# A filler that hands over from one part to the next within one request

## The chip, the cores and the metric

The kernel runs on one core of a Trainium2 chip. The core has five engines, each with its own instruction stream, which it works through in the order in which it was written: TensorE (PE; its weight loads are listed apart, as PEld), VectorE (DVE), ScalarE (ACT), GpSimd (POOL) and SyncE (SP). The metric is the device time of one execution in microseconds (us); lower is better.

## The reference

Attention over 2 batches of 8 heads (576 positions of 64), in which only scores within `tau` of a row's largest are kept; its output `x` (1152 rows of 512) goes through a first mixture of 8 experts and then a second of 4, each expert a hidden layer of 1024 with ReLU. Every expert sees every row:

```
scores = scale * np.matmul(q, k.transpose(0, 1, 3, 2))
thresh = np.max(scores, axis=-1, keepdims=True) - tau
scores = np.where(scores >= thresh, scores, -1000000000.0)
...
P = np.exp(logits)
for _ in range(8):
    P /= P.sum(1, keepdims=True) + 1e-09
    P /= P.sum(0, keepdims=True) + 1e-09
    P *= N / E
for e in range(E):
    h = np.maximum(x @ w1[e], 0.0)
    ye = h @ w2[e]
    out += P[:, e:e + 1] * ye
```

## The kernel before, in words

Everything is in one program, which writes each engine's instructions in a fixed order by hand. Products are taken in pieces: a float is split into a high part (`xh`, `wh`, `hh`, made by a cast on ACT) and the rest (`xl`, `wl`, `hl`, made by a subtract on DVE or POOL), and three products of such parts are summed.

**Attention.** 72 units of 128 query rows go through a pipeline; `Attention.step` writes one step of it: turns (transposes, L327 and L329) of the unit two steps back, the mask of the current one (L309 on DVE), the exponentials (L305 on ACT), `fill(0, ...)`, scores of the unit two steps on (L282), in some steps the product with the values (L383, L385), `fill(1, ...)`, and `side()`, which cooks weights: a cast on ACT (L107) and a subtract on POOL (L109) per tile. Units 0 to 15 and 16 to 35 belong to batch 0, the others to batch 1 (9 steps per pair of heads). Queries for a later head are prepared on ACT and POOL too (L252 to L257).

**The fill.** Once batch 0 is finished, its rows go through experts 0 and 1 of the first mixture while attention goes on for batch 1. `expert_fill` is a generator, called a part here: it yields after every few matmuls. A part covers 256 rows ("near") or 320 rows ("far"). First come 8 blocks, one per tile `ft` of the hidden layer: 12 matmuls into a bank of PSUM (L536), then `hh` on ACT (L542) and `hl` on DVE (L545), for a far part also copies of its edge columns on POOL (L549). A block takes three requests. Then for each 128 rows a product of 24 matmuls (L564), two to a request, whose bank is copied out at its end (L568). There are two banks for this and for the values' product. `todo` holds the parts in order: expert 0 near and far, expert 1 near and far. `pull(n)` takes `n` requests from the first; `fill` gives 3 in its first half of a step and the rest of a block (or 4 in all in the later products) in its second.

**After the attention** `todo` gets the near and far part of expert 1 for the first half of batch 1's rows ("chunk 2"), and a loop runs until `todo` is empty. An iteration has one `pull(3)`, and by its number `n`: from 18 on three ticks, in which POOL and ACT prepare weights for the main stage (sums L829, splits L80 and L85); up to 7, and then each third, a step of `gate()` (the mixture's weights: a small product on PE, L908, and eight small operations on DVE, L909 to L913 and L902 to L905); in the others sums of rows on DVE (L957 to L966), and, when the gate is done, two operations of `scale()` (L933, L935), which multiply the accumulators `acc` by these weights.

**The main stage** does all the rest by products of seven units per half expert. Its first half's units are taken in the order 1, 7, 6, 4, 5, 2, 3; unit 1 takes `xh` and `xl`, units 7, 6 and 4 take `xth` and `xtl`, made on ACT and DVE (L80, L85) at its start, and all are on PE's L1132. Operations of `scale()` that the loop has not got to are done in the main stage's slots.

Of the kernel before, what the change touches and what calls it, by code (L numbers as in the profile page):

```python
# [29 lines left out]
def attention_two_moe_kernel(ctx, tc, qP, kP, qT, kT, vp, tau, wg, w1, w1s, w2, w2s, dp, m2w1s, m2w2, m2w2s, out):  # L30
# [6 lines left out]
    def pool(stack, name, bufs=1, **kw):  # L37
        return stack.enter_context(tc.tile_pool(name=name, bufs=bufs, **kw))
# [39 lines left out]
    def split(eh, el, hi, lo, src):  # L78
        if eh is A:
            A.copy(hi, src)  # L80
        elif eh is V:
            V.tensor_copy(hi, src)
        else:
            G.tensor_scalar(hi, src, 1.0, 1.0, op0=ALU.mult, op1=ALU.mult)
        el.tensor_tensor(lo, src, f(hi), op=ALU.subtract)  # L85
# [6 lines left out]
    def fetch(n):  # L92
        while len(raws) < n and tiles:
            w, e, ft = tiles.pop(0)
            raw = rp.tile([P, DM], F32, tag="raw", name="raw", bufs=3)
            nc.sync.dma_start(raw, w[e, :, ft])
            raws.append(raw)

    def cook(later=None):

        k = 1 + len(cooked) // FT % 2
        if not len(cooked) % FT and len(cooked) < 2 * FT:
            gap(wp, 192 if k == 1 else 64)
        hi = wp.tile([P, DM], F32R, tag=f"w{k}h", name="wh", bufs=FT)
        lo = wp.tile([P, DM], F32R, tag=f"w{k}l", name="wl", bufs=FT)
        raw = raws.pop(0)
        A.copy(hi, raw)  # L107
        if later is None:
            G.tensor_tensor(lo, raw, f(hi), op=ALU.subtract)  # L109
        else:  # L110
            later.append(lambda: V.tensor_tensor(lo, raw, f(hi), op=ALU.subtract))
        cooked.append((hi, lo))
# [481 lines left out]
    with ExitStack() as att:  # L594
        ap = pool(att, "attn", side="right")
        ps_s = Ring([whole_psum[:, k:k + 2] for k in (0, 2)])
        ps_t = Ring([whole_psum[:, 4].rearrange("p (a b) -> p a b", a=4)])
        ps_r = Ring([whole_psum[:, 5]])
        banks.pool = ps = Some([whole_psum[:, k] for k in (6, 7)])
        at = Attention(ap, ps_s, ps_t, ps_r, ps)  # L600
        for p in range(H // 2):
            at.add_pair(0, p, 0, 256, True, p == 0)
        nA0 = len(at.units)
        for p in range(H // 2):
            at.add_pair(0, p, 256, 320, False)
        nA1 = len(at.units)
        for p in range(H // 2):
            at.add_pair(1, p, 0, S, False)
        at.plan()
        room = [2 * FT]  # L610
        at.load()
        drop = on[:, 0:1]
        V.tensor_scalar(drop, tau_sb, 0.0, None, op0=ALU.is_ge)
        V.tensor_scalar(esc, drop, 0.125, None, op0=ALU.mult)
        V.tensor_scalar(lin[:, 0:1], drop, -0.125, None, op0=ALU.mult)
        V.tensor_scalar(drop, drop, -BIG, BIG, op0=ALU.mult, op1=ALU.add)
        V.scalar_tensor_tensor(lin[:, 1:2], tau_sb, 8.0, drop, op0=ALU.mult, op1=ALU.add)
        V.tensor_tensor(drop, tau_sb, drop, op=ALU.add)
        V.tensor_scalar(on[:, 1:2], drop, -1.0, None, op0=ALU.mult)

        def side():
            if at.t >= -1:
                fetch(2)
            if at.t >= nA0 - 3 and raws and room[0] and (at.t % 3 < 2 if at.t < nA1 else room[0] > 2 or at.t % 2):
                room[0] -= 1
                cook()
            if at.t == 20:
                nc.sync.dma_start(wg_sb, wg)
                nc.sync.dma_start(dp_sb, dp)
            if at.t == 24:  # L630
                split(V, V, wg2[:, :, :E1], wg2[:, :, E1:], wg_sb)

        def free(n):
            room[0] += n

        X0, X1 = Expert(0), Expert(1)
        near, far = ((0, 0), (1, P)), ((2, 32), (3, 32 + P))
        todo = [(nA0 + 4, expert_fill(hp, X0, 0, 256, near, acc, None, 0, at.later, keep)),
                (nA1 + 3, expert_fill(hp, X0, 256, 320, far, acc, tail0[0], 0, at.later, free)),
                (nA1 + 3, expert_fill(hp, X1, 0, 256, near, y1, None, 0, at.later, keep)),  # L640
                (nA1 + 3, expert_fill(hp, X1, 256, 320, far, y1, tail0[1], 0, at.later, keep))]

        left, spent = [0], [0]
        few = dict(zip(range(nA1 - 3, nA1 + 4), (2, 2, 2, 2, 2, 1, 1)))

        def pull(n, end=True):

            for i in range(n):
                if not todo or at.t <= todo[0][0] or (left[0] == 1 and not end):
                    return i  # L650
                left[0] = next(todo[0][1], -1)
                if left[0] < 0:
                    todo.pop(0)
                if left[0] <= 0:
                    left[0] = 0
                    return i + 1
            return n

        def fill(phase, busy):
            if phase == 0:  # L660
                if 0 <= at.t < nA0 - 3 and at.t % 2 == 0:
                    room[0] -= 1
                    cook()
                spent[0] = pull(few.get(at.t, 3))
            elif left[0] or not busy:
                pull(max(few.get(at.t, RA1 if at.t < nA1 + 3 else RA2) - spent[0], 0), True)

        while at.step(fill, side):
            pass
        at.flush()  # L670
        while left[0]:
            pull(1)
        at.flush()
        while raws:
            cook()
            fetch(2)
# [917 lines left out]
```

## Time and profile before

| what | value |
|---|---|
| median of 3 runs (lowest to highest) | 1287.18 us (1287.1 to 1287.38) |
| the profiled execution's own time | 1286.37 us |
| its span | 1284.6 us |
| PE, PEld busy | 1267.8 us (99%), 1207.6 us (94%) |
| DVE, ACT, POOL busy | 880.5 us (69%), 736.4 us (57%), 897.7 us (70%) |
| bytes read, written | 69.86 MB, 2.36 MB |

The span is what the profiler saw from the first to the last instruction; the execution's own time has 1.8 us more around it. Busy time is the union of an engine's instructions. A row of a timeline gives start, length, engine, line of the kernel and operation; instructions of one kind that follow each other stand as one row with their count, and a bracket tells how long the engine had been idle before it and on whom it waited. In stretches the granted clock is a share of full speed.

### The profile page before, as it was taken

How to read it: one execution, taken by the hardware profiler on the slowest of the kernel's cores; microseconds unless marked ns; L12 is line 12 of the kernel's file. 1: busy time of each engine (PE TensorE's matmuls, PEld its weight loads, DVE VectorE, ACT ScalarE, POOL GpSimd, SP SyncE). 2: the span in 40 equal slices, each digit the busy share in tenths (PEclk: the TensorE clock that was granted, in tenths of full speed). 3: DMA queues.
4: the chain of work that ended last, by engine and by line, in shares of the span. 5: the costliest groups of instructions: out<-in, count | busy, mean ns of one | idle time of the engine just before them, and what ended most of it. 6: DMA issues, size and time to landing. Idle time of an engine off the chain costs nothing.

```text
span 1284.6 us, 25109 instructions
## 1 busy us (share of the span) xinstructions
PE 1267.8 (99%) x9373; PEld 1207.6 (94%) x9373; DVE 880.5 (69%) x1851; ACT 736.4 (57%) x1483; POOL 897.7 (70%) x987
## 2 busy tenths in 40 slices
PE   8998999999999999999999999999999999999998
PEld 5597988888889999999999999999989999999998
DVE  6888888666637666666666666666745666666667
ACT  6887887423446555555655555566546465555553
POOL 7997987405796767867776786777668568677770
PEclk9999999999999999999999999999999999999999
DMA  5542330101221112211111221111212012111102
GB/s 171 161 125 78 97 98 17 42 1 34 79 70 51 42 42 58 58 34 51 50 42 42 58 59 34 50 51 42 58 36 61 20 51 58 35 58 50 42 18 74
DMA packets 43225, 73.84 MB, mean 57 GB/s; under 512 B 5216, under 2 KB 12512, under 8 KB 43104
## 3 DMA queue, kind: packets, MB, share of 16 engines
q1 hardware_dynamic: 42816, 71.96, 19.4%
q8 instruction: 74, 1.21, 0.4%
q14 instruction: 47, 0.39, 0.1%
q10 hardware_dynamic: 288, 0.28, 0.1%
HBM read 69.86 MB, written 2.36 MB: 56 GB/s over the span
## 4 chain that ended last, share of the span: by engine, by line
PE 87%; DVE 5%; POOL 3%; issue 2%; ACT 2%; DMA 0%; SPq 0%; DVEq 0%; POOLq 0%; ACTq 0%
PE mm L1132 34%; PE mm L1444 33%; PE mm L564 5%; PE mm L536 5%; PE mm L282 2%; PE mm L1252 2%; PE mm L327 2%; DVE ex L309 1%; PE mm L376 1%; POOL wl L85 1%; DVE st L287 1%; PE mm L385 1%; DVE etl L358 1%; PE mm L383 1%; ACT ex L305 1%
## 5 line engine op out<-in xcount | busy, mean ns | idle before, releaser
L85 POOL TENSOR_TENSOR wl<-raw,wh 128x512 fp32r<-128x512 f32 x217 | 282.9, 1310 | 179.8 <-ACT wh L80 166.6
L1232 DVE SCALAR_TENSOR_TENSOR acc<-mm,p,acc 128x256 f32<-128x256 f32 (+1 forms) x428 | 195.3, 508 | 72.2 <-PE mm L1444 59.3
L1444 PE MATMUL mm<-wh,h 128*128 128x256 f32 x960 | 173.3, 279 | 0.0
L1139 ACT COPY snap<-mm 128x576 f32<-128x576 f32 x126 | 80.9, 642 | 157.1 <-DVE mm L1293 77.9
L80 ACT CAST wh<-raw 128x512 fp32r<-128x512 f32 x217 | 133.5, 627 | 47.3 <-PE mm L1444 26.4
L1444 PEld LDWEIGHTS mm<-wh,h 128*128 128x128 f32 x960 | 146.5, 188 | 0.0
L1132 PE MATMUL mm<-xh,wl 128*128 128x288 f32 x672 | 145.7, 298 | 0.3
L1132 PE MATMUL mm<-xh,wh 128*128 128x288 f32 x672 | 143.3, 294 | 0.0
L1132 PE MATMUL mm<-xl,wh 128*128 128x288 f32 x672 | 143.0, 294 | 0.0
L1444 PE MATMUL mm<-wl,h 128*128 128x256 f32 x480 | 134.5, 280 | 0.1
L1444 PE MATMUL mm<-wh,tails 128*128 128x256 f32 x696 | 126.1, 279 | 0.0
L85 POOL TENSOR_TENSOR wl<-sum,wh 128x512 fp32r<-128x512 f32 x82 | 107.1, 1307 | 8.2 <-ACT wh L80 8.1
L1132 PEld LDWEIGHTS mm<-xh,wl 128*128 128x128 f32 x672 | 106.3, 188 | 3.1 <-DVE mm L1152 0.5
L1132 PE MATMUL mm<-xth,wl 128*128 128x288 f32 x504 | 108.1, 295 | 0.1
L1132 PE MATMUL mm<-xtl,wh 128*128 128x288 f32 x504 | 107.7, 294 | 0.0
L1132 PE MATMUL mm<-xth,wh 128*128 128x288 f32 x504 | 107.5, 294 | 0.0
L1132 PEld LDWEIGHTS mm<-xl,wh 128*128 128x128 f32 x672 | 107.5, 188 | 0.0
L1132 PEld LDWEIGHTS mm<-xh,wh 128*128 128x128 f32 x672 | 107.3, 188 | 0.0
L1444 PEld LDWEIGHTS mm<-wh,tails 128*128 128x128 f32 x696 | 106.2, 188 | 0.0
L80 ACT CAST wh<-sum 128x512 fp32r<-128x512 f32 x82 | 51.5, 628 | 85.4 <-POOL sum L829 71.9
L1444 PE MATMUL mm<-wl,tails 128*128 128x256 f32 x348 | 97.2, 279 | 0.0
L1444 PEld LDWEIGHTS mm<-wl,h 128*128 128x128 f32 x480 | 90.1, 188 | 0.5 <-issue 0.3
(242 smaller groups left out, 3487.8 us busy)
## 6 DMA issues: line engine op xcount, KB each, us to landing
raw<-in_w1s SPq DMA_DIRECT2D x56, 256.0 KB, 2.6
raw<-in_w2s SPq DMA_DIRECT2D x48, 256.0 KB, 2.6
raw<-in_w SPq DMA_DIRECT2D x40, 256.0 KB, 3.2
raw<-in_m2w1s SPq DMA_DIRECT2D x32, 256.0 KB, 2.6
raw<-in_m2w2s SPq DMA_DIRECT2D x28, 256.0 KB, 2.7
kr<-in_kT SPq DMA_DIRECT2D x22, 288.0 KB, 3.0
vr<-in_vp SPq DMA_DIRECT2D x24, 160.0 KB, 2.3
qr<-in_qT SPq DMA_DIRECT2D x8, 288.0 KB, 2.9
```

The lines of the kernel that those rows point to most:

```text
L80: A.copy(hi, src)
L85: el.tensor_tensor(lo, src, f(hi), op=ALU.subtract)
L282: T.matmul(sc[:m, hf, :HS], lhsT=q, rhs=kk[:, hf * HS:(hf + 1) * HS], start=i == 0, stop=i == len(ops) - 1)
L287: V.tensor_reduce(st[:, 0:1], u["sc"][:, :, :HS], axis=AX.XY, op=ALU.max, negate=not u["q"][0][0]["ws"])
L327: T.transpose(et[:, kt], exf[:, kt * P:(kt + 1) * P], ident)
L536: T.matmul(ph[:, :n], lhsT=a[:, kt * P:(kt + 1) * P], rhs=x[:, kt, n0:n0 + n], start=i == 0 and kt == 0, stop=i == 2 and kt == KT - 1)
L564: T.matmul(py, lhsT=x, rhs=a, start=i == 0, stop=i == 3 * FT - 1)
L1132: T.matmul(ch[b][:, g, :HS], lhsT=w[:, (2 * g + kt) * P:(2 * g + kt + 1) * P], rhs=operand(u, kt, lo), start=first and j == 0, stop=j == l ...
L1139: A.copy(v[u], m)
L1232: V.scalar_tensor_tensor(a, src, s, a, op0=ALU.mult, op1=ALU.add)
L1252: T.matmul(py, lhsT=hid[x][:, kk, o:o + P], rhs=w[y], start=n == 0, stop=n == 3 * HF - 1)
L1444: T.matmul(m, lhsT=hid(x, kt + ko), rhs=wk[y], start=first and n == 0, stop=n == 5, skip_group_check=True)
```

## The change

Only `pull` is changed. When a part is at its end, its generator gives nothing more. Before, this was found out by a request, which was thereby used up, and `pull` returned. Now `pull` takes the part off `todo` and asks the next one within the same request, if that one's time has come. (The test of `end` goes too; no caller leaves it at a value at which it matters.)

```
         def pull(n, end=True):
 
             for i in range(n):
-                if not todo or at.t <= todo[0][0] or (left[0] == 1 and not end):
-                    return i
-                left[0] = next(todo[0][1], -1)
-                if left[0] < 0:
-                    todo.pop(0)
+                left[0] = -1
+                while left[0] < 0:
+                    if not todo or at.t <= todo[0][0]:
+                        left[0] = 0
+                        return i
+                    left[0] = next(todo[0][1], -1)
+                    if left[0] < 0:
+                        todo.pop(0)
                 if left[0] <= 0:
                     left[0] = 0
                     return i + 1
             return n
```

No instruction is added or removed, but many move. Lines behind the change have numbers higher by 3 in the changed program (L568 and before keep theirs). The first move is on PE, in step 40, between the turn of one unit and the scores of another; rows with a plus are new at their place, with a minus they stood there before.

```order
 L327 MATMUL mm_95<-ident_68,ex_1591 128x128 x4
 L329 MATMUL mm_95<-ident_68,ex_1591 64x128
+L536 MATMUL mm_95<-xh_90,wl_186 128x320 x4
+L536 MATMUL mm_95<-xl_91,wh_185 128x320 x4
+L536 MATMUL mm_95<-xh_90,wh_185 128x320 x4
 L282 MATMUL mm_95<-kh_1525,qs_1565 128x288 x2
 L282 MATMUL mm_95<-kl_1526,qs_1565 128x288 x2
```

The first block of the far part of expert 0 stands one step earlier than before; steps 55 and 70 get a block in the same way. The parts that follow a step 55 are two steps earlier, those that follow a step 70 three.

In the loop after the attention, ACT's order at the far part of chunk 2. Before:

```order
L80 CAST wh_3720<-raw1_3297 128x512
L80 CAST wh_3725<-raw3_3299 128x512
L568 COPY acc5_3282<-mm_95 128x512
L80 CAST wh_3739<-sum0_3301 128x512
L542 ACTIVATE hh_3765<-mm_95 128x320
L542 ACTIVATE hh_3785<-mm_95 128x320
L542 ACTIVATE hh_3805<-mm_95 128x320
L542 ACTIVATE hh_3834<-mm_95 128x320
```

And in the changed program, the fifth to the eighth block of the same part:

```order
L542 ACTIVATE hh_3819<-mm_95 128x320
L80 CAST wh_3827<-raw1_3342 128x512
L80 CAST wh_3832<-raw3_3344 128x512
L542 ACTIVATE hh_3851<-mm_95 128x320
L80 CAST wh_3859<-sum0_3346 128x512
L542 ACTIVATE hh_3876<-mm_95 128x320
L542 ACTIVATE hh_3905<-mm_95 128x320
```

The same casts stood ahead of all eight blocks and now stand between them; the cast of `sum0` is ahead of the seventh block's `hh`.

At the seam of the loop and the main stage, DVE's order behind the last scalings. Before (`acc8` is what the loop's last product is copied to):

```order
L935 SCALAR_TENSOR_TENSOR acc3_64<-y1_101,p1_86,acc3_64 128x512
L933 TENSOR_SCALAR acc7_3284<-acc7_3284,p1_86 128x512
L568 COPY acc8_3285<-mm_95 128x512
L933 TENSOR_SCALAR acc8_3285<-acc8_3285,p1_86 128x512
L85 TENSOR_TENSOR xtl_4039<-sums_3289,xth_4038 128x288 x6
```

And in the changed program:

```order
L936 TENSOR_SCALAR acc5_3327<-acc5_3327,p1_86 128x512
L568 COPY acc8_3330<-mm_95 128x512
L936 TENSOR_SCALAR acc6_3328<-acc6_3328,p1_86 128x512
L936 TENSOR_SCALAR acc7_3329<-acc7_3329,p1_86 128x512
L936 TENSOR_SCALAR acc0_61<-acc0_61,p1_86 128x512
L938 SCALAR_TENSOR_TENSOR acc0_61<-y1_101,p1_86,acc0_61 128x512
L936 TENSOR_SCALAR acc1_62<-acc1_62,p1_86 128x512
L938 SCALAR_TENSOR_TENSOR acc1_62<-y1_101,p1_86,acc1_62 128x512
L85 TENSOR_TENSOR xtl_4034<-sums_3334,xth_4033 128x288 x6
```

Between the copy of `acc8` and the six subtracts `xtl` stood one scaling and now stand six; five more follow behind `xtl`.

## Rows read from the trace of the kernel before

**Rows 1.** The page: busy time, the chain that ended last, POOL's largest group

```profile
PE 1267.8 (99%) x9373; PEld 1207.6 (94%) x9373; DVE 880.5 (69%) x1851; ACT 736.4 (57%) x1483; POOL 897.7 (70%) x987
...
PE 87%; DVE 5%; POOL 3%; issue 2%; ACT 2%; DMA 0%; SPq 0%; DVEq 0%; POOLq 0%; ACTq 0%
...
L85 POOL TENSOR_TENSOR wl<-raw,wh 128x512 fp32r<-128x512 f32 x217 | 282.9, 1310 | 179.8 <-ACT wh L80 166.6
```

**Rows 2.** Stretches: length, busy PE, PEld, DVE, ACT, POOL, clock, DMA, GB/s

```profile
126.89:157.40 30.51, 29.63 (x218) 29.36 (x219) 27.41 (x71) 26.00 (x59) 27.80 (x53) 1.00 0.28 80
...
241.10:321.85 80.75, 80.75 (x478) 70.96 (x478) 49.68 (x140) 22.20 (x56) 27.45 (x63) 1.00 0.09 30
```

**Rows 3.** PE's waits from 120 to 242 us: total, times, longest

```profile
PE mm L282 <- DVE ex L309: 1.5, 2, 1.0
PE mm L327 <- DVE etl L358: 1.5, 3, 0.9
```

**Rows 4.** Timeline of step 40

```profile
126.69 0.57 ACT L568 COPY acc<-mm 128x512 f32<-128x512 f32 x1
...
127.77 0.53 PE L282 MATMUL mm<-kh,qs 128*128 128x288 f32 x2 [1.03 <-DVE ex L309]
```

**Rows 5.** Timeline of step 64: PE's product, the last weights' subtract

```profile
209.72 0.39 PE L564 MATMUL mm<-wh,hl 128*128 128x512 f32 x1
...
210.25 1.29 POOL L109 TENSOR_TENSOR wl<-raw,wh 128x512 fp32r<-128x512 f32 x1
```

**Rows 6.** The chain that ended last, 284 to 300 us

```profile
283.94 3.43 PE mm L564 x15
...
290.36 0.17 PE mm L908 x2
290.53 5.33 PE mm L536 x36
```

**Rows 7.** Timeline of chunk 2's far blocks

```profile
294.62 0.62 ACT L80 CAST wh<-sum 128x512 fp32r<-128x512 f32 x1 [2.77 <-POOL sum L829]
...
295.15 1.18 ACT L542 ACTIVATE hh<-mm 128x320 fp32r<-128x320 f32 x3
...
295.62 1.29 DVE L545 SCALAR_TENSOR_TENSOR hl<-mm,hh 128x320 fp32r<-128x320 f32 x3 [0.29 <-ACT hh L542]
...
296.82 0.23 DVE L909 TENSOR_REDUCE mm<-mm 128x8 f32<-128x72 f32 x1
...
298.32 0.39 POOL L549 TENSOR_SCALAR tails<-hh 128x32 fp32r<-128x32 f32 x2
...
298.55 0.23 DVE L905 TENSOR_TENSOR p<-p,mm 128x72 f32<-128x72 f32 x1
```

**Rows 8.** Timeline of the scalings and the start of the main stage

```profile
313.18 0.48 DVE L933 TENSOR_SCALAR acc<-acc,p 128x512 f32<-128x512 f32 x1
...
313.69 0.75 DVE L935 SCALAR_TENSOR_TENSOR acc<-y,p,acc 128x512 f32<-128x512 f32 x1
...
322.06 0.69 DVE L568 COPY acc<-mm 128x512 f32<-128x512 f32 x1 [4.39 <-PE mm L564]
...
322.78 0.49 DVE L933 TENSOR_SCALAR acc<-acc,p 128x512 f32<-128x512 f32 x1
...
323.18 2.30 DVE L85 TENSOR_TENSOR xtl<-sums,xth 128x288 fp32r<-128x288 f32 x6
...
323.70 0.76 PE L1132 MATMUL mm<-xtl,wh 128*128 128x288 f32 x2
```

**Rows 9.** Timeline: subtracts on DVE without and beside one on POOL

```profile
281.99 0.46 DVE L964 TENSOR_TENSOR sums<-sums,extra 128x288 f32<-128x288 f32 x1
...
290.15 1.51 POOL L85 TENSOR_TENSOR wl<-sum,wh 128x512 fp32r<-128x512 f32 x1
...
290.55 1.44 DVE L964 TENSOR_TENSOR sums<-sums,extra 128x288 f32<-128x288 f32 x1
```

## The prediction

> **What bounds the kernel now.** The page first: TensorE is busy 1267.8 of 1284.6 us, and the chain that ended last runs through it for 87% of the span [rows 1]. Then the stretches: in the 30.5 us of attention from step 40 on, PE is busy 29.63 us, and in the 80.75 us between 241.10 and the main stage it is busy all of the time, both at granted clock 1.00 [rows 2]. PE's instructions run in the order in which they are written, the change leaves their number and shapes as they are, so the time moves only where PE waits. Its waits in the attention's second half are two entries, 1.5 us and 1.5 us [rows 3]; from 241 on the view of waits names none. So 3.0 us is all that a better dealt fill can win, and every wait that the new order makes is a loss.
>
> **What the change moves.** A part is eight blocks of 12 matmuls (L536) and then its products (L564). Before, the end of a part used up a request, and a step got nothing: steps 40, 55 and 70 of the attention and three iterations of the loop after it. After, those three steps carry a block each. From step 40 the fill runs one step ahead, from 55 two, from 70 three: three blocks of 320 columns leave the time after the attention. One costs 5.33/3 = 1.78 us of PE [rows 6], so 5.33 us move forward, and the total stays. The loop ends after 41 iterations instead of 48, because it also loses its empty ones; its per-iteration work (the gate, the sums, the ticks that prepare weights) keeps its iteration numbers, and so meets other fill. Four places follow.
>
> **A. The steps that were empty (gain).** Step 40: PE waits 1.03 us for the mask (L309) [rows 4]; step 55: the 0.9 us for L358 that are the longest of the second entry of [rows 3]; step 70: a part of the 0.6 us that this entry leaves, 0.2 by thirds. With a block of 1.78 us ahead of them, these waits are covered. But a hand-over also takes the bank that the product just ended in: step 40's block can start only when ACT has copied it, 126.69 + 0.57 = 127.26, and PE goes on at 127.77 now [rows 4], so of the 1.03 us only 0.51 are won. At step 68, which now also hands over, PE has little more than the turn to do during the same copy of 0.57 us; I put 0.2 on it. Bounds: 0.5 to 3.0 us won; I take 0.5 + 0.9 + 0.2 - 0.2 = 1.4.
>
> **B. The last weights of expert 1 (cost).** Expert 1's first product moves from steps 64-66 to 62-64, and ends with the eighth tile of its second weights. That tile is cooked by `side` of step 63, as before, and its subtract on POOL (L109) ran from 210.25 to 211.54, behind the next head's queries on POOL. PE stands at the place of step 64 where it now needs it at 209.72 [rows 5]. By these rows PE waits 1.8 us; it may be less because ACT and DVE carry no block's copies in that step (0.39 and 0.43 us, as `hh` and `hl` in [rows 7]). Bounds 0 to 1.8; I take 1.4, near the row.
>
> **C. The gate in the loop (cost).** Chunk 2's far blocks were iterations 28 to 35 and become 21 to 28, while the weights' preparation stays at iterations 20 to 26. ACT and POOL now interleave the two. In the old order ACT waited 2.77 us with the cast of the sum behind POOL, then did three `hh` in a row, with DVE's three `hl` after them [rows 7]; PE never noticed, as it had work. In the new order `hh` of the seventh block stands behind that cast, its `hl` behind it on DVE, and the gate's eight small operations of iteration 27 behind this `hl`; PE's L908 of iteration 30 waits for the last. From the start of the first block: PE reaches that L908 after eight blocks and twelve products, 8 x 1.78 + 12 x 3.43/15 = 17.0 us, and three gate steps' matmuls at 0.17 [rows 6]: 17.5. POOL: the second block's copies end at 5.2 (two blocks 3.56, `hh` 1.18/3, `hl` 1.29/3, copies of both 0.39 each [rows 7]); then come seven subtracts and sums, 1.31 us [rows 1] to 1.51 us [rows 9] each (I lay out 1.39), and the copies of two blocks: 5.2 + 9.7 + 1.6 = 16.5. Then the cast 0.62, `hh` 0.39, `hl` 0.43, the gate's chain from 296.82 to 298.55 + 0.23, 1.96 [rows 7], and four times the passing from engine to engine, 0.08 by `hh` and `hl` (295.15 + 0.39 against 295.62): 20.2. PE waits 20.2 - 17.5 = 2.7 us; with 1.31 it is 2.1, with 1.51 3.5, and two of POOL's seven done before the second block's copies would leave nothing. I take 2.7, bounds 0 to 4.
>
> **D. The start of the main stage (cost).** Before, DVE had finished scaling all rows but the last when PE ended its products: behind the copy of acc8 at 322.06 stood one L933, and from 323.18 the six subtracts `xtl`, 2.30 us in all [rows 8]. PE's second unit needs the first two of them, and met them at 323.70 with a wait of a few tenths. After, only two scalings stand ahead of the acc8 copy and six between it and `xtl`: four L933, two L935. L933 takes 0.48 us and L935 0.75 [rows 8]: 4 x 0.48 + 2 x 0.75 - 0.49 (the one of before) = 2.9 us later. PE has one unit of work ahead of that and nothing to put between, so it waits 2.9 us at the least. The rest of the scalings (five) falls behind `xtl`, where DVE had 3 us idle.
> The upper bound: moved by 2.9 us, all of `xtl` runs beside POOL's subtracts. A subtract of 288 columns took 0.46 us with POOL idle and 1.44 us beside one of POOL [rows 9]. Two such `xtl` are needed before PE's unit can go on: 2.9 + 2 x (1.44 - 0.46) = 4.8 us. I take 4.0, between the ends, nearer the upper because POOL's subtract began 3 us after PE's last product and the moved `xtl` do too.
> The Trainium skill (GPSIMD Engine Reference, section 1, Specifications) has a rule on that: GpSimd shares its SBUF interfaces with VectorE and contends with VectorE instructions that have two SBUF inputs. Both kinds stand here, and the trace agrees (1.44 against 0.46 us). By the rule the term is at its upper end, 4.8 us, and the sum 0.8 us higher; without it 2.9, and 1.1 us lower.
>
> **The sum.** -1.4 + 1.4 + 2.7 + 4.0 = +6.7 us. The profiled execution took 1286.37 us, so 1293.1; the median of the runs is 0.81 us above it: **1293.9 us**. What can be told from no change is 0.2%, 2.6 us: 1284.6 to 1289.75.
>
> **Rivals.**
> *The start of the main stage alone.* POOL gets the sum done in time and the last weights come early enough: C and B fall away, -1.4 and D's 2.9 to 4.0 remain, +1.5 to +2.6: 1288.7 to 1289.8 us. For it: POOL is busy less than TensorE, and both C and B rest on an order of ten operations laid out by hand; against it: every wait of B is in measured rows. 0.22, of which 0.17 within 0.2%.
> *Faster: the moved blocks ride for free.* If the attention's steps are set by DVE (27.41 of 30.51 us busy [rows 2]) and PE's busy time there hides stalls, steps 40 to 75 do not get longer for the three blocks, and all of the 5.33 us that leave the tail are won instead of 1.4. It becomes faster by over 0.2% from the point where B, C and D together cost less than 5.33 - 2.6 = 2.7 us; with D at its lower bound, 2.9, and B and C at nothing, it is 1287.18 - 5.33 + 2.9 = 1284.75 us, just at that point, and any part of D that PE doesn't see puts it beyond. Against it: PE's waits in these steps are 3.0 us, so its row of busy time would have to be wrong by as much again. 0.07, of which 0.05 faster and 0.02 within.
> *The waits cost the clock too.* A wait of 3 to 4 us at D could lower the granted clock. The rows show 1.00 in every stretch read [rows 2]. If it fell to its lower level, 1.2 GHz, 3 us of matmuls would take 6, and the forecast would come to 1296.9 us. The Trainium skill (TensorE: Matmul & The Clock Gate, "What's actually happening") has it that an idle TensorE is throttled; no stretch of [rows 2] holds such a fall. 0.05, slower.
> *No effect.* The rate of the fill falls out the same (the last part of a step still lost): the order of the changed program speaks against it. 0.02, within.
> *The forecast* with its own range, +3.5 (B and C at half, D at 2.9, A as taken) to +10.1 (B, C and D at their upper bounds, A at 0.5): 1290.7 to 1297.3 us. 0.64, slower.
>
> **How the numbers follow.** The likeliest case gives 1293.9. The range 1288.4 to 1297.3 holds most of the forecast (0.60 of 0.64), nearly all of the first rival and a part of the clock's. It leaves out the faster case. Faster 0.05; within 0.2% 0.17 + 0.02 + 0.02 = 0.21; slower the rest, 0.74.
>
> **What would show it.** A: PE's waits at L282 and L327 in steps 40 and 55 gone or under half, and a wait for ACT's L568 in step 40. B: PE waiting for `wl` of L109 at L564, in a step without a block. C: a PE wait for `p` of L905 at an L908, just after the first products of chunk 2's far part, 2 to 3 us. D: PE waiting for `xtl` at L1135 (L1132 before) for 3 to 5 us, directly after the last product. After that the main stage should be shifted and otherwise alike. The prediction is wrong if the view of waits shows neither C nor D, or if steps of the attention get longer than the block they carry.

## The result, and the profile after

The changed kernel takes 1299.12 us (median of 4 runs, 1298.84 to 1300.63) against 1287.28 us of the kernel before: a ratio of 1.0094 with a 95% interval of 1.0082 to 1.0107, 11.8 us slower. The forecast was 1293.9 us, the range ended at 1297.3.

The page of the changed kernel: busy time, the granted clock in 40 slices, the chain that ended last.

```profile
PE 1273.6 (98%) x9373; PEld 1212.5 (93%) x9373; DVE 882.0 (68%) x1851; ACT 736.6 (57%) x1483; POOL 899.6 (69%) x987
...
PEclk9999999999899999999999999999999999999999
...
PE 85%; DVE 7%; ACT 3%; POOL 2%; issue 1%; DMA 0%; DVEq 0%; ACTq 0%; POOLq 0%
```

Against [rows 1] PE has the same number of instructions and is busy 5.8 us longer, in a span that is 12.9 us longer. So not all of the loss is waiting: the same matmuls took longer somewhere, and the one slice with a lower clock (the eleventh, 324 to 357 us) shows one of the places. PE's waits from step 40 to the main stage's first units, in total, times and longest:

```profile
PE mm L1135 <- DVE xtl L85: 4.4, 1, 4.4
PE mm L911 <- DVE p L908: 3.1, 1, 3.1
PE mm L564 <- POOL wl L109: 0.9, 1, 0.9
PE mm L536 <- ACT acc L568: 0.6, 1, 0.6
PE mm L282 <- DVE ex L309: 0.5, 1, 0.5
PE mm L327 <- DVE etl L358: 0.4, 1, 0.4
```

The two entries of [rows 3] have shrunk from 3.0 to 0.9 us, and four are new. The timeline of the two long ones, with the engines that each hangs on:

```profile
307.49 0.62 ACT L80 CAST wh<-sum 128x512 fp32r<-128x512 f32 x1 [3.72 <-POOL sum L832]
...
308.01 0.76 ACT L542 ACTIVATE hh<-mm 128x320 fp32r<-128x320 f32 x2
...
308.47 0.49 DVE L545 SCALAR_TENSOR_TENSOR hl<-mm,hh 128x320 fp32r<-128x320 f32 x1 [3.42 <-ACT hh L542]
...
308.88 0.23 DVE L912 TENSOR_REDUCE mm<-mm 128x8 f32<-128x72 f32 x1
...
310.89 0.44 PE L911 MATMUL mm<-p,ones 128*128 128x72 f32 x2 [3.08 <-DVE p L908]
...
327.31 0.69 DVE L568 COPY acc<-mm 128x512 f32<-128x512 f32 x1 [2.87 <-PE mm L564]
...
327.92 1.27 DVE L936 TENSOR_SCALAR acc<-acc,p 128x512 f32<-128x512 f32 x3
...
330.12 3.04 POOL L85 TENSOR_TENSOR wl<-raw,wh 128x512 fp32r<-128x512 f32 x2 [3.46 <-ACT wh L80]
...
330.41 1.63 DVE L938 SCALAR_TENSOR_TENSOR acc<-y,p,acc 128x512 f32<-128x512 f32 x1
...
331.96 3.35 DVE L85 TENSOR_TENSOR xtl<-sums,xth 128x288 fp32r<-128x288 f32 x6
...
333.53 0.97 PE L1135 MATMUL mm<-xtl,wh 128*128 128x288 f32 x2 [4.41 <-DVE xtl L85]
...
335.26 0.68 PE L1135 MATMUL mm<-xtl,wh 128*128 128x288 f32 x2
```

The upper five rows are term C link by link: POOL's sum, ACT's cast, `hh`, `hl`, the gate's eight operations, PE. The lower ones are term D: where [rows 8] has one scaling between the copy of acc8 and `xtl`, there are six, and the second L938 took 1.63 us beside POOL's subtract. The last row shows a third thing: a pair of matmuls takes 0.68 us instead of 0.43. The same stretches by busy time (the last three columns are clock, DMA share, GB/s):

```profile
307.60:310.80 3.20, 0.21 (x1) 0.00 (x0) 2.08 (x10) 1.82 (x5) 3.20 (x8) 1.00 0.30 79
310.80:315.50 4.70, 4.61 (x15) 3.65 (x16) 3.93 (x12) 0.00 (x0) 3.61 (x12) 0.65 0.37 106
315.50:328.80 13.30, 13.30 (x66) 11.22 (x65) 5.66 (x22) 3.69 (x9) 1.31 (x1) 0.99 0.06 18
328.80:333.40 4.60, 0.32 (x3) 0.08 (x1) 4.53 (x6) 1.68 (x3) 3.04 (x2) 0.93 0.19 38
333.40:339.60 6.20, 6.07 (x25) 5.99 (x26) 4.62 (x11) 1.42 (x3) 1.91 (x2) 0.50 0.21 62
```

Around each of the two stretches in which PE stood, the granted clock fell to its lower level of 1.2 GHz (0.50): in part of the 4.7 us behind the first, and in the last 0.8 us of the second wait and all of the 6.2 us behind it. Then it came back.

From the start times of the instructions the loss can be dealt out; "after" is how much later the changed kernel starts the same one:

| at the | before, us | after | of it |
|---|---|---|---|
| mask of step 40 (L309, on DVE) | 126.89 | +0.14 | not the change |
| last matmul of the gate's first product (PE) | 255.15 | +7.16 | 30 matmuls of L564 more are done by then, 30 x 0.232 = 6.97; so attention +0.05 |
| last matmul of the loop's products (PE) | 321.62 | +5.26 | 5.26 - 0.19 = 5.07 for C: 3.1 wait, 1.55 the lower clock, 0.4 around them |
| first of the second layer (PE, L1252) | 333.58 | +12.37 | 7.11 for D: 4.4 wait, 2.5 the lower clock, 0.2 around them |
| end of the span | 1284.58 | +12.89 | 0.5 over the whole main stage |

The share of the clock is read twice. At C, the profile of e8_busy (below) has the same wait of 3.1 us and no fall, and is 3.52 us behind where the changed kernel is 5.07: the fall costs 1.55 us. At D, the 24 matmuls from the end of the wait on start over 6.04 us (333.53 to 339.57), and over 3.50 us in the kernel before (323.70 to 327.20): 2.5 us.

### The profile page after: what moved, and what is told of

Read it like the earlier page. It is cut to its first block, busy times and chain, and to the rows that moved or that the text cites. A ratio compares the mean times of both kernels' runs of the same rounds, so it can differ in the third digit from the quotient of the medians.

```text
span 1297.5 us, 25098 instructions
## 1 busy us (share of the span) xinstructions
PE 1273.6 (98%) x9373; PEld 1212.5 (93%) x9373; DVE 882.0 (68%) x1851; ACT 736.6 (57%) x1483; POOL 899.6 (69%) x987
## 4 chain that ended last, share of the span: by engine, by line
PE 85%; DVE 7%; ACT 3%; POOL 2%; issue 1%; DMA 0%; DVEq 0%; ACTq 0%; POOLq 0%
PE mm L1135 36%; PE mm L1447 33%; PE mm L564 4%; PE mm L536 3%; PE mm L1255 3%; DVE ex L309 2%; PE mm L282 2%; DVE st L287 2%; PE mm L376 1%; PE mm L327 1%; ACT ex L305 1%; POOL wl L85 1%; PE mm L385 1%; DVE hl L545 1%; DVE etl L358 1%
```

## The experiments

Each time is a median, each ratio is against the runs of the kernel before on the same chip (1286.9 to 1287.0 us), with its 95% interval. In all but one it is the changed kernel that is edited.

**Which hand-overs do it.** `e1_attention_only` and `e2_loop_only` keep the hand-over in one of the two places (where `over[0]` is true); elsewhere a part's end uses up a request:

```
                     left[0] = next(todo[0][1], -1)
                     if left[0] < 0:
                         todo.pop(0)
+                        if not over[0]:
+                            break
```

> The hand-over within a request holds in the attention alone; in the loop after it a part's end uses up a request, as before. Theory (each wait comes from what the order puts ahead of it, and TensorE's clock falls after a wait of about 3 us): the attention gives +0.2 us, as in the changed kernel; five scalings instead of six stand ahead of the six xtl, so PE waits 3.9 to 4.2 us there and the clock falls after it (2.6 us more); the far blocks meet the weights one iteration later than in the changed kernel, so the gate's wait is 0 to 2 us, without a fall. Sum +6.7 to +9 us on the kernel before: 1294 to 1296 us. Rival (the hand-overs in the loop alone do the harm): 1287.5 us.

> The hand-over within a request holds in the loop alone; the attention is dealt as before. All scalings but one stand ahead of the copy of acc8, as before, and only the first far block's hh stands ahead of the last cast of the weights' preparation. Theory (what counts is what stands ahead of xtl and of the gate's operations): no wait at either place, the clock stays at 1.00, -0.3 to +0.5 us on the kernel before: 1287.0 to 1287.8 us. Rival (the loop's hand-overs do the harm): 5 us or more above the kernel before.

Measured: e1 1294.06 us, 1.0054 [1.0041, 1.0066]; a wait of 4.1 us for `xtl` with the fall of the clock, 0.3 us at the gate. e2 1287.73 us, 1.0006 [0.9997, 1.0015]; no wait that the kernel before doesn't have but 0.2 us at the gate. PE's waits behind the attention in e1, and then in e2:

```profile
PE mm L1138 <- DVE xtl L85: 4.1, 1, 4.1
PE mm L913 <- DVE p L910: 0.3, 1, 0.3
```

```profile
PE mm L913 <- DVE p L910: 0.2, 1, 0.2
```

So the attention's hand-overs alone make D, though behind the attention: they take fill out of the loop, and the loop's side work finds less to hide behind. They are 7.1 of the 11.8 us. Those in the loop alone cost nothing that can be told. C, with its wait of 3.1 us, is in neither: it takes both.

**Order alone.** `e7_before_scale_late` edits the kernel before:

```
-        elif not gated and l1[0] >= FT:
+        elif not gated and l1[0] >= FT and n >= 46:
             for _ in range(2):
                 next(sl, None)
```

> The kernel before, with the scalings of acc held back in the loop until its iteration 46, which gives on DVE the order of the changed kernel at the seam: two scalings, the copy of acc8, six scalings, then the six xtl. Nothing else is changed, and no part hands over. Theory (that order alone makes the wait and the fall of the clock): a PE wait of 4.4 us for xtl, then a clock of 1.2 GHz for some 5 us: 1287.3 + 7.0 = 1294.3 us. Rival (the wait also needs the earlier fill): 1287.3 to 1290 us.

Measured: 1293.73 us, 1.0052 [1.0040, 1.0065], a wait of 4.4 us for `xtl` and a clock of 0.62 in the 8 us around it (the entry of the waits, then the window, columns as above):

```profile
PE mm L1132 <- DVE xtl L85: 4.4, 1, 4.4
...
324.00:332.00 8.00, 3.71 (x15) 3.64 (x16) 7.89 (x13) 2.07 (x5) 3.02 (x2) 0.62 0.21 68
```

Six scalings between the copy of acc8 and `xtl` make D (6.7 of its 7.1 us) without any hand-over.

**The clock.** `e8_busy` gives PE work where it waited:

```
                 wh, wl = need(0, 7 * i + n)
+                if i == 0 and u == 7 and g == 0:
+                    idle = banks.pool.single()
+                    for j in range(34):
+                        T.matmul(idle[:, :HS], lhsT=xh[:, 0, :P], rhs=xh[:, 1, :HS], start=True, stop=True)
+                    banks.pool.give(idle)
```

> The changed kernel with 34 matmuls of 288 columns more, written to a spare bank and never read, just ahead of the unit that waits for xtl: they take 34 x 0.132 = 4.5 us, so PE is busy where it waited. Theory (the clock falls because PE stood still): no wait for xtl is left, or some tenths, the clock stays at 1.00 behind the seam, and 2.6 us are won though work was added: 1296.5 us. Rival (the clock falls there for another reason, or the loss behind the seam is another wait): 1299.1 us or more.

Measured: 1297.48 us, 1.0077 [1.0065, 1.0090]. Windows of its profile, columns as above, at the gate's wait and at the seam, and the rows of the added matmuls and of the next wait:

```profile
308.00:316.00 8.00, 5.17 (x24) 4.31 (x25) 6.27 (x21) 1.94 (x6) 6.34 (x16) 1.00 0.26 78
...
324.00:332.00 8.00, 7.98 (x56) 7.46 (x54) 6.23 (x9) 1.68 (x3) 4.18 (x3) 1.00 0.19 65
```

```profile
327.07 4.64 PE L1136 MATMUL mm<-xh 128*128 128x288 f32 x34
...
341.54 0.53 PE L1140 MATMUL mm<-xh,wl 128*128 128x288 f32 x2 [1.35 <-DVE mm L1160]
```

With PE busy over the place of the wait, the clock stays at 1.00 at the seam: the fall came from standing still. The gain is 1.6 us and not 2.6, since DVE, still as late, now makes PE wait 1.3 us a little further on. What the theory had not foreseen is the first window: the gate's wait was 3.1 us as ever, and this time no fall followed. Of the five executions two had a mean clock of 1.000 (1296.15 and 1296.44 us) and three of 0.998 (1297.5 to 1297.7 us): so here the clock falls in some executions, at a price of 1.3 us. That it falls behind the wait of 3.1 us in those three is inferred, as only one execution is profiled; four other profiles (the changed kernel, e3, e9, e10) show a fall behind such a wait.

**POOL beside DVE.** `e9_hush` holds the preparation of weights back for eight slots of the main stage (a counter in `tick`, set behind the loop):

```
         clock[0] += 1
-        if agenda and ...
+        hush[0] -= 1
+        if hush[0] < 0 and agenda and ...
```

> The changed kernel with the preparation of weights held back for the first eight slots of the main stage, so that no subtract of POOL runs beside the scalings and the xtl there. Theory (of the 4.4 us, 2.9 are the operations ahead, and 1.5 the slowing of DVE's two-input operations beside POOL): the wait is 2.9 to 3.1 us, the fall of the clock after it stays or is shorter: 1297 to 1297.8 us, if the weights held back are not missed later. Rival (POOL's neighbourhood costs nothing): wait 4.4 us, 1299.1 us.

Measured: 1296.80 us, 1.0074 [1.0061, 1.0086]. Its waits from 300 to 400 us:

```profile
PE mm L914 <- DVE p L911: 3.1, 1, 3.1
PE mm L1139 <- DVE xtl L85: 2.5, 1, 2.5
PE mm L1139 <- POOL wl L85: 0.9, 2, 0.7
```

4.4 us became 2.5: of the wait for `xtl` 1.9 us were the neighbourhood of POOL (the second L938 took 0.75 us here and the six `xtl` 2.29), and the weights held back cost 0.9 us later. (The Trainium skill, GPSIMD Engine Reference, section 1, Specifications, names the cause as interfaces to SBUF that GpSimd shares with VectorE; the trace agrees, 1.63 against 0.75 us for the same operation.)

**The gate's wait.** `e4_ticks_9` and `e4_ticks_29` move the preparation of weights ahead of the far blocks, or behind them (`if n >= 18` becomes 9, or 29).

> The changed kernel, with the preparation of weights in the loop begun at iteration 9 instead of 18, so that all its casts on ACT stand ahead of the far blocks of chunk 2 and none between them. Theory (the gate's chain is late because the seventh block's hh stands behind the cast that waits for POOL): the gate's wait of 3.1 us and the fall of the clock after it (1.7 us) go, the wait for xtl and its fall stay: 1299.1 - 4.8 = 1294.3 us. Rival (the gate's chain is late on DVE in any case, since eight operations of 2 us and the blocks' hl have to fit): a wait of 1 us or more stays, 1295.5 to 1299 us.

> The changed kernel, with the preparation of weights in the loop begun at iteration 29 instead of 18, behind the last far block of chunk 2. Begun at iteration 9 it had moved the wait at the gate and not removed it: there DVE's sums ran beside POOL's subtracts, three of them in 3.88 us. Behind the blocks neither the casts nor those sums meet POOL's work. Theory (the gate's chain is late by ACT's casts that wait for POOL, or by DVE's sums beside POOL): no wait at the gate, no fall of the clock there, the wait for xtl and its fall stay: 1299.1 - 4.8 = 1294.3 us. Rival (the gate's chain is late by the number of its operations beside the blocks): a wait of 1 us or more stays, 1295.5 us or more.

Measured: 1296.66 us, 1.0080 [1.0067, 1.0093], with a gate's wait of 2.0 us, as the rival had it; and 1295.66 us, 1.0068 [1.0055, 1.0081], with no gate's wait (the last product of the loop stands 0.2 us behind that of the kernel before, for C had been 5.07) but 6.0 us for `xtl`. Each moved POOL's work to another place, and there it met DVE. Timeline of the first, then of the second:

```profile
286.79 3.88 DVE L960 TENSOR_TENSOR sums<-xh,xl 128x288 f32<-128x288 f32 x3
...
294.06 0.44 PE L911 MATMUL mm<-p,ones 128*128 128x72 f32 x2 [2.03 <-DVE p L908]
```

```profile
322.87 3.84 DVE L936 TENSOR_SCALAR acc<-acc,p 128x512 f32<-128x512 f32 x3
...
323.56 4.30 POOL L85 TENSOR_TENSOR wl<-raw,wh 128x512 fp32r<-128x512 f32 x3
...
330.02 0.98 PE L1135 MATMUL mm<-xtl,wh 128*128 128x288 f32 x2 [5.96 <-DVE xtl L85]
```

Three scalings that took 1.27 us in the changed kernel take 3.84 us here.

**Scalings left to the main stage.** `e3_scale_later` takes the branch with `next(sl, None)` out of the loop; `e5_both_9` also starts the preparation at iteration 9.

> The changed kernel, with no scaling of acc in the loop: all nine are left to the main stage's slots, so nothing stands between the copy of acc8 and the six xtl. Theory (xtl is late by the scalings ahead of it, and the second fall of the clock follows that wait): the wait of 4.4 us and the fall after it (2.6 us) go, the gate's wait of 3.1 us with the fall after it stays: 1299.1 - 7.0 = 1292.1 us. Rival 1 (xtl is late by what POOL does beside it): a wait of 1.5 us or more stays, 1293.5 to 1295. Rival 2 (the clock falls there for another reason): 1294.7 us, with a clock of about 0.6 behind the seam.

> The changed kernel with both edits: no scaling in the loop, and the preparation of weights begun at iteration 9. Theory: both long waits go and with them both falls of the clock; what is left is the attention's +0.2 us: 1287.2 to 1287.6 us, clock 1.00 throughout. Rival (the waits were not all of it, the hand-overs cost something in the main stage too): 1288.5 us or more.

Measured: 1300.28 us, 1.0104 [1.0090, 1.0118], and 1298.60 us, 1.0090 [1.0075, 1.0106]. Both theories failed, and so did e3's rivals; e5's rival has the time right (1288.5 us or more), but e5 waits 7.5 us for L1152, as e3 does. Timeline of e3:

```profile
329.90 7.34 DVE L936 TENSOR_SCALAR acc<-acc,p 128x512 f32<-128x512 f32 x5
...
340.46 0.76 DVE L1141 TENSOR_TENSOR mm<-snap,mm 128x576 f32<-128x576 f32 x1
...
344.25 0.85 PE L1132 MATMUL mm<-xh,wl 128*128 128x288 f32 x2 [7.72 <-DVE mm L1152]
```

The wait for `xtl` is gone, and one of 7.7 us has come 10 us later: nine accumulators' scalings stand behind `xtl` on DVE, five operations take 7.34 us beside POOL, and L1141 and L1152, which free PE's banks, stand behind them. The step of the theory that fell is that work put behind the waiting place costs nothing.

**Towards a repair.** `e6_repair` (with the preparation at iteration 29) and `e12_gate` (where it was) let the gate end earlier, `e10_cook` cooks the last weights of expert 1 a step earlier, `e11_best` is e6 with e10's edit:

```
-        if n < 7 or n % 3 == 0 and gated:
+        turn_of_gate = n % (2 if l1[0] >= FT else 3) == 0 and gated
+        if n < 7 or turn_of_gate:
...
-            ... else room[0] > 2 or at.t % 2):
+            ... else room[0] > 2 or at.t % 2 or at.t == 62):
```

(The first pair is the gate's, the second the cooking's. The branch behind the gate's takes the new condition too.)

> The changed kernel with the preparation of weights begun at iteration 29, and with a step of the gate in each second iteration instead of each third, once the far blocks are done, so that the gate ends some three iterations earlier and all scalings but one stand ahead of the copy of acc8, as in the kernel before. Theory (two waits and the two falls of the clock behind them are the whole loss; scalings left to the main stage only moved it): both go, what stays is the attention's +0.2 us: 1287.0 to 1287.6 us at a clock of 1.00. Rival (the shorter loop has too little room for this work wherever it stands): a wait of 2 us or more somewhere between the far blocks and the main stage's first products, 1289.5 us or more.

> The changed kernel, with the last tile of expert 1's weights cooked one step earlier (step 62 instead of 63), so that its subtract stands ahead of the next head's queries on POOL. Theory (PE's wait of 0.9 us in step 64 is for that subtract): the wait goes, 1299.1 - 0.9 = 1298.2 us, or a part of it moves to the scores that wait for the queries. Rival (attention is late there in any case): 1299.1 us.

> The kernel of e6_repair with the earlier cooking of e10_cook. Theory: PE's waits in the attention's second half are 1.5 us where they were 3.0 in the kernel before, and no other is new: 1285.6 to 1286.6 us, the first version that beats the kernel before, by 0.5 to 1.5 us. Rival (what is won in the attention is lost behind it): 1287 us or more.

> The changed kernel with a step of the gate in each second iteration instead of each third once the far blocks are done, and the preparation of weights where it was (from iteration 18 on). All scalings but one stand ahead of the copy of acc8, and POOL's subtracts are over when they begin. Theory (xtl is late by the scalings ahead of it, and in the repair the scalings were slow because POOL worked beside them): the wait for xtl and the fall of the clock behind it go, the gate's wait of 3.1 us and its fall stay: 1299.1 - 7.0 = 1292.1 us. Rival (too little room in the shorter loop for DVE's work, wherever it stands): a wait of 2 us or more for xtl, or gate waits of that size behind the blocks, 1295 us or more.

Measured: e6 1298.70 us, 1.0091 [1.0077, 1.0105], wait for `xtl` 7.8 us, with the scalings slow beside POOL as in e4_ticks_29. e10 1297.86 us, 1.0080 [1.0067, 1.0094]: PE's wait for L109 is gone, and at the gate's first product the kernel is 1.35 us earlier than the changed one; 0.16 of that it had already at step 40, so the cooking wins 1.2 us, more than the wait of 0.9 us. e11 1298.13 us, 1.0089 [1.0075, 1.0102], likewise with 8.0 us for `xtl`. e12 1298.72 us, 1.0093 [1.0080, 1.0107], with three waits of about 1 us for `xtl` in place of the 4.4 and a gate's wait of 5.8 us: PE now came to a gate step one iteration earlier than DVE, which still stood behind ACT's late cast.

Then the attention's hand-over alone with the earlier gate (e13), with the earlier cooking (e14), with acc7 scaled last but one (e15: `left = [4, 5, 6, 0, 1, 2, 3, 7, 8]`), and with the preparation held back for four slots (e16):

> The hand-over in the attention alone, as in e1_attention_only, with the gate's steps of e12_gate. In e1_attention_only the gate's wait was 0.3 us and the wait for xtl 4.1 us with a fall of the clock. Theory: the wait for xtl and the fall go, no wait of over 0.5 us is left behind the attention: 1294.1 - 6.6 = 1287.5 us. Rival (too little room): 1289.5 us or more.

> e13_attention_gate with the last tile of expert 1 cooked one step earlier, which in e10_cook won 1.3 us up to the loop's start. Theory: 1287.5 - 1.3 = 1286.2 us, the first version that beats the kernel before (by 0.7 us). Rival (what the attention wins is lost behind it): 1287 us or more.

> e14_attention_gate_cook, with acc7 scaled behind acc3 instead of ahead of acc0, so that DVE does not stand on the copy of acc7. Theory (lateness by 1.2 us is enough to bring xtl beside POOL): the copy of acc8 follows PE's last product at once, xtl comes as early as in the kernel before, and the wait of 3.1 us shrinks to 0.5 us or less: 1290.1 - 2.8 = 1287.3 us, at most 0.3 us above the kernel before, 0.8 us below it where no main-stage wait is new. Rival (POOL works beside xtl in any case, since this kernel's weights run ahead): a wait of 2 us or more, 1289 us or more.

> e15_order, with the preparation of weights held back for the first four slots of the main stage. Theory (with xtl early, POOL comes behind it anyway): as e15_order within 0.5 us. Rival (POOL beside xtl is what is left): at least 1.5 us faster than e15_order, 1286.3 us, the first to beat the kernel before, unless the weights held back are missed later (0.9 us in e9_hush).

Measured: e13 1291.27 us, 1.0034 [1.0022, 1.0047]; e14 1290.09 us, 1.0025 [1.0015, 1.0035]; e15 1286.38 us, 0.9996 [0.9987, 1.0004]; e16 1289.86 us, 1.0021 [1.0012, 1.0030]. e13 and e14 came out as their rivals had it, with three waits of about 1 us for `xtl` each, e15 as its theory had it, e16 as neither. The timeline of e14 at the seam:

```profile
316.36 0.88 DVE L938 TENSOR_SCALAR acc<-acc,p 128x512 f32<-128x512 f32 x2 [3.18 <-ACT acc L568]
...
323.56 5.24 DVE L85 TENSOR_TENSOR xtl<-sums,xth 128x288 fp32r<-128x288 f32 x5
...
324.06 0.78 PE L1139 MATMUL mm<-xtl,wh 128*128 128x288 f32 x2 [1.02 <-DVE xtl L85]
...
324.10 2.91 POOL L85 TENSOR_TENSOR wl<-raw,wh 128x512 fp32r<-128x512 f32 x2 [3.30 <-ACT wh L80]
...
327.38 0.40 PE L1139 MATMUL mm<-xtl,wh 128*128 128x288 f32 x1 [1.06 <-DVE xtl L85]
```

and that of e15:

```profile
321.43 0.69 DVE L568 COPY acc<-mm 128x512 f32<-128x512 f32 x1 [2.92 <-PE mm L564]
...
322.56 2.30 DVE L85 TENSOR_TENSOR xtl<-sums,xth 128x288 fp32r<-128x288 f32 x6
...
323.07 0.76 PE L1139 MATMUL mm<-xtl,wh 128*128 128x288 f32 x2
```

In e14 DVE stood 3.2 us on the copy of acc7, so `xtl` came 1 us too late, met POOL, and five of them took 5.24 us. In e15 it comes in time, ahead of POOL, and PE doesn't wait. Holding POOL back as well (e16) won nothing there and made PE wait 2.1 us later on, with a fall of the clock behind it. So there is room enough in a loop that is shorter by the three blocks, if the order of the side work is made for it. With e2, e15 is the only version whose interval holds 1, and the only such one that hands over in the attention; its 0.6 us can't be told from no change. The same order with the loop's hand-overs too wasn't tried.

## Why the prediction was wrong, point by point

- *What bounds the kernel*: right. PE's waits and the clock behind them moved the time, but for 0.5 us spread over the main stage, whose cause stays open.
- *A, the steps that were empty*: the waits for L309 and L358 fell from 3.0 to 0.9 us and that for the bank came in step 40 (0.6 us), as laid out, so 1.5 us were won by the view of waits, against 1.4. In step 40 alone next to nothing was won instead of 0.5: L282 starts there 1.70 us later, for a block of 1.78.
- *B, the last weights*: PE waited at the place named, 0.9 us instead of 1.4. The late weights cost more than that wait, though: without them (e10) the attention is 1.2 us shorter. Counted from step 40, its last matmul (L385) is 5.32 us later than in the kernel before, with three blocks, 5.33 us, more done. So A and B cancel as forecast, at 1.2 us each instead of 1.4. That the moved blocks ride for free is refuted by the same 5.32 us.
- *C, the gate*: right in every link; 3.1 us instead of 2.7.
- *D, the seam*: right in its place and cause (e7); 4.4 us instead of 4.0. It was set between 2.9 and 4.8 by the neighbourhood of POOL (2.9 + 2 x 0.98 is 4.9, in fact), and e9 shows 2.5 without it. The slowing fell on a scaling too (the second L938, 1.63 us instead of 0.75), and not on `xtl` alone.
- *The clock*: this is the step that failed. It stood among the rivals, with a chance of 0.05, 3 us, and at D alone; the sum put it at nothing. No row carried the 3 us; 2.5 were measured there. It fell at both waits in the profile, and the mean clock of 0.996 is the same in each of the four executions. It cost 1.55 us at C and 2.5 us at D, 4.1 of the 11.8 us. Without them the measured time would be 1295.0 us, inside the range. With C and D forecast as waits of 2.7 and 4.0 us and all earlier stretches at 1.00, the rows had no wait of that length to read a price from, which was a reason to widen the range, not to leave the fall out. The Trainium skill (TensorE: Matmul & The Clock Gate, "HAM oscillation — how this bites in real kernels") tells of a kernel that pays for the return to the full clock after each wait for data. The trace agrees, with one return for each of the two waits (clock 0.65 in the 4.7 us behind one, 0.50 in the 6.2 us behind the other).
- The terms add up: 0.05 for the attention, 3.1 and 4.4 of waits, 4.1 of clock, 0.6 around the waits, 0.5 in the main stage and 0.14 ahead of the change are the 12.9 us of the span.

## What to carry to other kernels

Where PE is busy 99% of the time, filling its idle slots wins at most what its waits add up to (here 3.0 us), while work taken forward leaves other engines' work uncovered later: before such a change, look at what is done beside the work that leaves. Operations that an engine works through in a fixed order delay what stands behind them; moving the scalings behind `xtl` was as bad as leaving them ahead. And a single wait of PE of 2 us or more is to be priced with the slower matmuls that can follow it (here 1.55 us behind one of 3.1, 2.5 behind one of 4.4).

## What the runs showed of the hardware that was not expected

- The granted clock fell at waits of 4.1 us and more in each profile, at a wait of 3.1 us in four profiles and not in a fifth (e8_busy), at one of 2.0 us in one profile and not in another (e4_ticks_9, e5_both_9), and not at three of about 1 us each within 7.3 us (e14, clock 1.00).
- Operations on DVE with one tensor from SBUF slow down beside POOL too: a scaling of 128x512 took 0.42 us alone (1.27/3) and 1.28 us beside POOL's subtracts (3.84/3). I had put the price on operations with two inputs alone [rows 9].
